# A fused attention and two-MLP kernel: block products in phases of 4, 4 and 6 units, sums on VectorE, weight sums split later

## The chip, the cores and the metric

One Trainium2 chip, one core. The metric is the device time of one execution in microseconds (us). TensorE multiplies (PE in the rows; PEld its weight loads), VectorE (DVE), ScalarE (ACT) and GpSimd (POOL) do the rest, SyncE (SP) issues the DMAs. Each engine works through its own queue in order.

## The reference, cut to what matters

```python
def reference(q, k, v, moe_w_in, moe_w_out, moe2_w_gate, moe2_w_val, moe2_w_out, moe2_rms_g):
    x = attention(q, k, v)              # 4 x 8 heads, 576 tokens, window 128, distance bias
    x = heads_joined(x)                 # 2304 tokens x 512
    h = x @ moe_w_in                    # 512 x 2048
    x = (h * np.clip(h + 3, 0, 6) / 6) @ moe_w_out
    xn = x / np.sqrt(np.mean(x * x, -1, keepdims=True) + 1e-6) * moe2_rms_g
    g = xn @ moe2_w_gate                # 512 x 1536
    return (g / (1 + np.exp(-g)) * (xn @ moe2_w_val)) @ moe2_w_out
```

## The kernel before, in words

All products run in float32r on TensorE, and every operand is given as a high part (a rounded copy, made by ScalarE) and a low part (operand minus high part, made by VectorE). A product of two such pairs is three matmuls: high by high, high by low, low by high.

**First MLP with attention.** Six blocks of 384 tokens; a slot per 128 columns of the hidden layer, in which attention steps of a later block, ten to twenty matmuls each, are mixed in. In parts 3 to 5 of it (blocks 2 to 4; p in the code) most slots end with a *turn* of the second MLP's weights (`W2.turn`): a piece of 128x512 comes as 64-bit words, is converted by `convert` on VectorE and ScalarE, and goes back to DRAM: the two input matrices as they are (kinds 0 and 1), the output matrix (kind 2) split into high and low. When both pieces of a pair of output-weight chunks are there, GpSimd forms four sums of their halves (S1 to S4), and in the next two turns ("late") ScalarE and VectorE split these and SyncE stores them. `TURNS` holds the order of the pieces; a pair of chunks takes six turns, and two extra turns stand in part 5.

**Second MLP.** Tokens come in three sets of 768 (s = 0, 1, 2), the hidden layer in twelve chunks of 128; a *group* i = 12 s + m is one chunk of one set, 36 in all. A group computes gate and value by seven block products of six matmuls each (a form of Strassen's method, Winograd's), into three PSUM banks; the banks alternate between even and odd groups. Its steps, in code order: product 0, ScalarE copies it (`s1`, line 919); product 1, VectorE adds (`u`, line 922); product 2 on top of product 0, ScalarE's Silu (925); product 3 on top of product 1, VectorE adds (928); product 4, VectorE (931); product 5, which overwrites the bank of products 1 and 3, VectorE (933), Silu (934); product 6, VectorE (937) and the multiplication 938, which gives the group's hidden values g. So product 2 waits for `s1`, product 3 for the add of 922, product 5 for that of 928, product 6 for that of 931.

Other work is placed by `job(i, place, ...)` at fixed places of group i: "start", "silu" (behind line 925), "sum" (behind 928), "silu 2" (behind 934), "end" (behind 938), or a number, which is a unit of the phase or outputs behind the group.

Set 0's output product is plain (`outputs`, behind groups 2, 4, 6, 8, 11 and 12). The input weights' block operands are made during the last part of the first MLP and groups 2 to 8 (`Parts`: load, four GpSimd sums, high, low, stores). Sets 1 and 2 have their output product in *rounds* of four groups, six rounds, 0 to 5, again by seven block products: SEQUENCE c a g b e f d, each of one factor from the weights (A.. or S.., fetched from DRAM into three rooms in turn, line 1069) and one from g (B.. or T..). T1 to T4 are differences of g's blocks (`Round.sum`, line 1054); each block's high part is line 1057, its low part line 1060; p is the half of the round's groups it comes from (0: the first two, 1: the last two). A *unit* is one block product for one half d of the output columns: six matmuls (line 1076), then an eviction into a running total: ScalarE copies in a set's first round (1105), VectorE adds otherwise (1107; e and f always). b adds into a's PSUM tile and d into e's. A round's units run in two phases: eight behind its sixth following group (c a g b, behind i0 + 5), six behind i0 + 7 (e f d). Behind the last group the last round's 14 units run in a row. After a unit pair the factor three places further in SEQUENCE is fetched. `ROUND_JOBS` and `FINAL_JOBS` (last round) place the sums and parts, relative to i0 + 4. At the end of a set, adds of totals and the stores follow (1123, 1126), on GpSimd for set 1 and VectorE for set 2.

In the trace group 8 begins at 634.0 us, 13 at 696.2, 14 at 703.5, 16 at 718.3, 17 at 726.5, 24 at 823.9, 28 at 874.3, 35 at 960.7.

## Time and profile before

| | |
|---|---|
| median of 3 runs | 998.02 us (997.67 to 998.17) |
| the profiled execution | 998.81 us, its span 996.8 us |
| TensorE, matmuls | 941.9 us busy, 94% |
| VectorE | 687.1 us, 69% |
| ScalarE | 478.0 us, 48% |
| GpSimd | 253.0 us, 25% |
| mean granted TensorE clock | 0.987 |

The span runs from the first to the last instruction; the time also holds what lies around it. Busy shares are means over stages with different limits, so a wait must be looked at in its own stage. A clock of 1.0 is 2.4 GHz, and the other level, 1.2 GHz, shows as a mean below 1.0 where it held for a part of a stretch.

### The profile page before, as it was taken

How to read it: one execution, taken by the hardware profiler on the slowest of the kernel's cores; microseconds unless marked ns; L12 is line 12 of the kernel's file. 1: busy time of each engine (PE TensorE's matmuls, PEld its weight loads, DVE VectorE, ACT ScalarE, POOL GpSimd, SP SyncE). 2: the span in 40 equal slices, each digit the busy share in tenths (PEclk: the TensorE clock that was granted, in tenths of full speed). 3: DMA queues.
4: the chain of work that ended last, by engine and by line, in shares of the span. 5: the costliest groups of instructions: out<-in, count | busy, mean ns of one | idle time of the engine just before them, and what ended most of it. 6: DMA issues, size and time to landing. Idle time of an engine off the chain costs nothing.

```text
span 996.8 us, 15304 instructions
## 1 busy us (share of the span) xinstructions
PE 941.9 (94%) x5408; PEld 844.2 (85%) x5408; DVE 687.1 (69%) x1433; ACT 478.0 (48%) x1049; POOL 253.0 (25%) x390
## 2 busy tenths in 40 slices
PE   7899999999989999989999999999989888988897
PEld 4677888888877888878998999998979888988887
DVE  6788666556878778876567657777545677564667
ACT  6799556455556556654455444331224332223231
POOL 4333022232324344333323323200020202050210
PEclk9899999999999999999999999999999999999999
DMA  7546211024666574761454778675785565666526
GB/s 237 185 166 243 116 38 41 30 70 143 211 220 209 173 228 144 248 213 74 148 201 187 276 260 317 238 273 195 272 300 192 192 212 204 243 240 216 208 85 211
DMA packets 90860, 190.79 MB, mean 191 GB/s; under 512 B 6432, under 2 KB 66848, under 8 KB 87584
## 3 DMA queue, kind: packets, MB, share of 16 engines
q1 hardware_dynamic: 90784, 189.82, 55.1%
q8 instruction: 42, 0.69, 0.3%
q14 instruction: 34, 0.28, 0.1%
HBM read 139.46 MB, written 50.33 MB: 190 GB/s over the span
## 4 chain that ended last, share of the span: by engine, by line
PE 67%; DVE 14%; ACT 7%; DMA 5%; issue 4%; POOL 2%; SPq 0%; ACTq 0%; DVEq 0%; POOLq 0%
PE ps_o L559 14%; PE ps_h L546 14%; PE ps_o L911 9%; PE ps_y L1076 6%; PE ps_S L911 5%; PE ps_A L911 5%; PE ps_y L961 5%; PE ps_h L911 3%; DMA u<-w 3%; PE ps_av L480 2%; DVE u L1060 2%; DMA wraw<-w 2%; PE ps_t L462 2%; DVE wx L187 1%; PE ps_s L419 1%
## 5 line engine op out<-in xcount | busy, mean ns | idle before, releaser
L559 PE MATMUL ps_o<-w,g 128*128 128x512 f32 x864 | 225.6, 404 | 2.0 <-DVE w L191 1.8
L546 PE MATMUL ps_h<-xs,w 128*128 128x384 f32 x1152 | 220.5, 339 | 2.1 <-DVE t L786 2.0
L546 PEld LDWEIGHTS ps_h<-xs,w 128*128 128x128 f32 x1152 | 202.3, 188 | 8.9 <-DVE t L786 3.3
L559 PEld LDWEIGHTS ps_o<-w,g 128*128 128x128 f32 x864 | 157.3, 189 | 41.4 <-issue 5.6
L786 DVE SCALAR_TENSOR_TENSOR t<-t,ps_h 128x384 f32<-128x384 f32 x96 | 53.0, 552 | 92.5 <-ACT t L785 92.5
L1054 POOL TENSOR_TENSOR u<-u 128x384 f32<-128x384 f32 x33 | 39.2, 1207 | 247.6 <-DVE u L1054 237.9
L1076 PE MATMUL ps_y<-u 128*128 128x384 f32 x424 | 85.3, 340 | 6.0 <-DMA u<-w 6.0
L785 ACT ACTIVATE t<-ps_h,three 128x384 f32<-128x384 f32 x96 | 55.2, 575 | 74.6 <-PE ps_h L546 68.5
L911 PE MATMUL ps_o<-S,tw 128*128 128x384 f32 x336 | 69.6, 351 | 15.1 <-DVE u L922 14.8
L1076 PEld LDWEIGHTS ps_y<-u 128*128 128x128 f32 x424 | 75.2, 191 | 8.2 <-issue 4.5
L911 PEld LDWEIGHTS ps_o<-S,tw 128*128 128x128 f32 x336 | 61.8, 196 | 17.5 <-DVE u L922 16.9
L448 ACT ACTIVATE t<-t,m 128x128 f32<-128x128 f32 (+1 forms) x144 | 61.2, 427 | 31.0 <-DVE t L440 15.9
L791 ACT CAST g<-t 128x384 fp32r<-128x384 f32 x96 | 49.3, 514 | 52.3 <-DVE t L786 50.7
L934 ACT ACTIVATE r<-r 128x384 f32<-128x384 f32 x36 | 18.9, 526 | 115.6 <-DVE r L933 115.6
L450 POOL TENSOR_SCALAR r<-den 128x2 f32<-128x2 f32 x72 | 27.7, 385 | 180.5 <-ACT t L448 178.5
L797 DVE TENSOR_TENSOR g<-t,g 128x384 fp32r<-128x384 f32 x96 | 57.2, 596 | 22.8 <-ACT g L791 22.5
L469 POOL TENSOR_SCALAR_AFFINE_SELECT pt<-pt 128x256 f32<-128x256 f32 x82 | 36.1, 442 | 89.2 <-ACT pt L467 86.4
L451 POOL TENSOR_TENSOR r<-r,minus 128x2 f32<-128x2 f32 x72 | 56.4, 783 | 6.0
L1060 DVE TENSOR_TENSOR u<-u 128x384 fp32r<-128x384 f32 x64 | 42.2, 688 | 14.6 <-ACT u L1057 14.5
L961 PE MATMUL ps_y<-wo,g 128*128 128x512 f32 x216 | 50.0, 389 | 0.0
L462 PE MATMUL ps_t<-ident,t 128*128 128x128 f32 x190 | 35.5, 290 | 13.9 <-DVE t L456 7.2
L180 ACT ACTIVATE wx<-wraw 128x512 f32<-128x512 f32 (+1 forms) x52 | 42.7, 821 | 11.5 <-DMA wraw<-w 11.5
(169 smaller groups left out, 1744.2 us busy)
## 6 DMA issues: line engine op xcount, KB each, us to landing
tw<-t SPq DMA_DIRECT2D x52, 896.0 KB, 6.3
wraw<-w SPq DMA_DIRECT2D x36, 512.0 KB, 4.6
wraw<-w SPq DMA_DIRECT2D x16, 1024.0 KB, 9.1
u<-s SPq DMA_DIRECT2D x48, 256.0 KB, 5.5
t<-th SPq DMA_DIRECT2D x12, 896.0 KB, 4.1
t<-tl SPq DMA_DIRECT2D x12, 896.0 KB, 4.2
u<-w SPq DMA_DIRECT2D x36, 256.0 KB, 4.0
b<-wx SPq DMA_DIRECT2D x24, 256.0 KB, 3.6
```

The source lines that it names most:

```text
L448: act.activation(p, p, AF.Exp, bias=self.m[:, a : a + 1], scale=-1.0, accum_out=self.den[:, a : a + 1])
L451: pool.tensor_tensor(self.r, self.r, minus, ALU.pow)
L462: pe.transpose(self.ps[:, a, c], self.t[:, a, c * P : (c + 1) * P], ident)
L546: pe.matmul(ps[:, : n * P], lhsT=w[:, a, c * P : (c + 1) * P], rhs=xs[c][:, b, : n * P], start=(k == 0), stop=(k == 3 * KC - 1),)
L559: pe.matmul(o, lhsT=g[:, a, i * P : (i + 1) * P], rhs=w[:, b], start=(m == first and a == 0 and b == 0), stop=(m == last and a == 1),)
L785: act.activation(r[:, :nq], ps[:, :nq], AF.Relu, bias=three)
L786: vec.scalar_tensor_tensor(out=r[:, :nq], in0=r[:, :nq], scalar=6.0, in1=ps[:, :nq], op0=ALU.min, op1=ALU.mult)
L797: vec.tensor_sub(g[:, 1, :nq], r[:, :nq], f32(g[:, 0, :nq]))
L911: pe.matmul(ps, lhsT=w[a][:, k, c * P : (c + 1) * P], rhs=x[:, b, c], start=(start and j == 0), stop=(j == 5), skip_group_check=True,)
L961: pe.matmul(ps, lhsT=gs[i + k][:, a, t // 3, t % 3 * P : (t % 3 + 1) * P], rhs=wo[i + k][:, b], start=(k == 0 and a == 0 and b == 0), stop ...
L1060: vec.tensor_sub(self.part(name, p, 1), self.at(name, p), f32(self.part(name, p, 0)))
L1076: pe.matmul(ps, lhsT=w[:, p, a, d * P : (d + 1) * P], rhs=self.part(name, p, b), start=(p == j == 0 and k not in CHAINED), stop=(p == 1 an ...
```

## The change

Five things are changed.

- A round's units run in three phases: c and g behind group i0 + 5, a and b behind i0 + 6, e, f and d behind i0 + 7. c and a change their PSUM tiles with each other's kind: c, a, b, e, d use the fixed pair, g and f the pair of the next group's banks.
- All sums of g (T1 to T4) are on VectorE; none is left on GpSimd. The places of sums and parts are new, and the rooms of the parts (`slot`) follow them.
- The sums of the output weights are stored unsplit in the first MLP. In the second, behind the "end" of groups 4 to 15 one is loaded (`load_sum`), and at "silu" of groups 5 to 16 it is split and stored (`split_sum`). The two extra turns go, and `TURNS` begins each pair of chunks with the output weights.
- The last round runs a b, c g, e f d; of set 1's and set 2's last adds, C12's is on GpSimd.
- Some steps of the operands of set 2 (`turn(s)` with s = 1) move by a place or two.

```diff
+TURNS = [(m + i, k) for m in range(0, M2, 2) for i, k in ((0, 2), (0, 0), (1, 2), (0, 1), (1, 0), (1, 1))]
+FACTORS = {"c": ("S4", "B22"), "g": ("S3", "T3"), "a": ("A11", "B11"), "b": ("A12", "B21"), "e": ("S1", "T1"), "f": ("S2", "T2"), "d": ("A22", "T4")}
+SPLIT_AT = 5
 ROUND_JOBS = {
...
-    (0, "silu"): [("sum", "vec", "T1", 0), ("sum", "vec", "T1", 1), ("sum", "pool", "T3", 0), ("sum", "pool", "T3", 1), ("high", "B21", 0), ("high", "B21", 1)],
+    (0, "silu"): [("sum", "T3", 0), ("sum", "T3", 1), ("low", "B22", 1), ("high", "T3", 0), ("high", "T3", 1)],
...
-UNITS = {5: "c0 c1 a0 a1 g0 g1 b0 b1".split(), 7: "e0 e1 f0 f1 d0 d1".split()}
+UNITS = {5: "c0 c1 g0 g1".split(), 6: "a0 a1 b0 b1".split(), 7: "e0 e1 f0 f1 d0 d1".split()}
...
         def turn(self):
-            late, self.late = self.late[:1], self.late[1:]
-            for m, parity, x in late:
-                t = wcpool.tile([P, 2, DM], F32R, tag="wt", name="w", bufs=1)
-                act.copy(t[:, 0], x)
-                vec.tensor_sub(t[:, 1], x, f32(t[:, 0]))
-                sp.dma_start(out=self.sums[m][:, parity], in_=f32(t))
...
                 run.send(t)
-                self.begin()
+                if m % 2 == 0:
+                    self.begin()
                 next(run)
...
-                    self.late = [(m // 2, i, x) for i, x in enumerate(self.x)]
+                    for parity, y in enumerate(self.x):
+                        sp.dma_start(out=self.sum32[m // 2][:, parity], in_=y)
                     self.x = []
+                    self.begin()
+
+        def load_sum(self, i):
+            self.late[i] = ypool.tile([P, DM], F32, tag="y", name="ws")
+            sp.dma_start(out=self.late[i], in_=self.sum32[i // 2][:, i % 2])
+
+        def split_sum(self, i):
+            x = self.late.pop(i)
+            high, low = (ypool.tile([P, DM], F32R, tag="y", name="wt") for _ in range(2))
+            act.copy(high, x)
+            vec.tensor_sub(low, x, f32(high))
+            for k, y in enumerate((high, low)):
+                sp.dma_start(out=self.sums[i // 2][:, i % 2, k], in_=f32(y))
...
-            if not last and (p == 3 and m > 3 or p > 3 and m % 4 != 2 or p == 5 and m in (2, 6)):
+            if not last and (p == 3 and m > 3 or p > 3 and m % 4 != 2):
                 W2.turn()
...
-        def sum(self, on, name, p):
+        def sum(self, name, p):
...
-            on.tensor_sub(self.at(name, p), self.at(a, p), self.at(b, p))
+            vec.tensor_sub(self.at(name, p), self.at(a, p), self.at(b, p))
...
+        def order(self):
+            return [SEQUENCE[k] for k in ((2, 3, 0, 1, 4, 5, 6) if self.final else range(7))]
...
-                    p, tag = own[k not in CHAINED.values()][d]
+                    p, tag = own[k in "gf"][d]
...
-                            on.tensor_add(total(x, d), total(x, d), total("V", d))
+                            (pool if x == "C12" else on).tensor_add(total(x, d), total(x, d), total("V", d))
...
-            job(i + 9, 5, x.later, "S4", 2)
-            job(i + 9, 6, x.high, 1)
-            job(i + 10, "silu 2", x.later, "S3", 3)
-            job(i + 10, "end", x.low, 1)
+            job(i + 9, 3, x.later, "S4", 2)
+            job(i + 9, 3, x.high, 1)
+            job(i + 10, "silu 2", x.low, 1)
+            job(i + 10, 3, x.later, "S3", 3)
...
+    for i in range(M2):
+        job(SPLIT_AT - 1 + i, "end", W2.load_sum, i)
+        job(SPLIT_AT + i, "silu", W2.split_sum, i)
...
-    for off in UNITS:
+    for off in (6, 5, 7):
         x.phase(off, x.i0 + off)
```

Where instructions stand now is shown at three places. The first is ScalarE in group 8, from the copy `s1` on (`th` is a high part of the input weights); before:

```order
L919 COPY s_7007<-ps_h 128x384
L948 CAST g<-t 128x768
L925 ACTIVATE r<-ps_h 128x384
L316 CAST th<-tx 128x1024
L934 ACTIVATE r<-r 128x384
L316 CAST th<-tx 128x768
```

and now:

```order
L938 COPY s_7003<-ps_h 128x384
L967 CAST g<-t 128x768
L944 ACTIVATE r<-ps_h 128x384
L335 CAST th<-tx 128x1024
L308 CAST wt<-ws 128x512
L953 ACTIVATE r<-r 128x384
```

The cast of a weight sum (`wt` from `ws`) stands behind the one of `th`. VectorE in the same group, before:

```order
L922 TENSOR_TENSOR u<-s_7007,ps_A 128x384
L950 TENSOR_TENSOR g<-t,g 128x768
L928 TENSOR_TENSOR u<-s_7007,ps_A 128x384
L931 TENSOR_TENSOR t<-u,ps_S_7006 128x384
L933 TENSOR_TENSOR r<-u,ps_A 128x384
```

and now:

```order
L941 TENSOR_TENSOR u<-s_7003,ps_A 128x384
L969 TENSOR_TENSOR g<-t,g 128x768
L309 TENSOR_TENSOR wt<-ws,wt 128x512
L947 TENSOR_TENSOR u<-s_7003,ps_A 128x384
L950 TENSOR_TENSOR t<-u,ps_S_7002 128x384
L952 TENSOR_TENSOR r<-u,ps_A 128x384
```

The subtraction of that split stands between the group's first two adds (922 and 928 before, 941 and 947 now).

The second place is VectorE from the end of group 16 to the first add of group 17 (low parts are `u<-u` of line 1060, now 1084; a sum is line 1054, now 1078); before, while GpSimd has its six sums in the same stretch:

```order
L928 TENSOR_TENSOR u<-s_7713,ps_A 128x384
L931 TENSOR_TENSOR u<-u,ps_S_7712 128x384
L933 TENSOR_TENSOR r<-u,ps_A 128x384
L1060 TENSOR_TENSOR u<-u 128x384 x2
L937 TENSOR_TENSOR u<-u,ps_S_7712 128x384
L938 TENSOR_TENSOR u<-u,r 128x768
L1060 TENSOR_TENSOR u<-u 128x384 x3
L922 TENSOR_TENSOR u<-s_7797,ps_o_7795 128x384
```

and now:

```order
L947 TENSOR_TENSOR u<-s_7777,ps_A 128x384
L950 TENSOR_TENSOR u<-u,ps_S_7776 128x384
L952 TENSOR_TENSOR r<-u,ps_A 128x384
L956 TENSOR_TENSOR u<-u,ps_S_7776 128x384
L957 TENSOR_TENSOR u<-u,r 128x768
L1084 TENSOR_TENSOR u<-u 128x384 x2
L941 TENSOR_TENSOR u<-s_7858,ps_o_7856 128x384
```

Two low parts stand between the multiplication and the next group's first add instead of three. The third place is VectorE from group 34 on; before, group 35 follows at once:

```order
L928 TENSOR_TENSOR u<-s_9586,ps_A 128x384
L931 TENSOR_TENSOR u<-u,ps_S_9585 128x384
L933 TENSOR_TENSOR r<-u,ps_A 128x384
L1060 TENSOR_TENSOR u<-u 128x384 x2
L937 TENSOR_TENSOR u<-u,ps_S_9585 128x384
L938 TENSOR_TENSOR u<-u,r 128x768
L1060 TENSOR_TENSOR u<-u 128x384
L1054 TENSOR_TENSOR u<-u 128x384
L922 TENSOR_TENSOR u<-s_9663,ps_o_9661 128x384
```

and now, with the evictions of a0 a1 b0 b1 (line 1135) behind it:

```order
L947 TENSOR_TENSOR u<-s_9617,ps_A 128x384
L950 TENSOR_TENSOR u<-u,ps_S_9616 128x384
L952 TENSOR_TENSOR r<-u,ps_A 128x384
L1078 TENSOR_TENSOR u<-u 128x384
L1084 TENSOR_TENSOR u<-u 128x384 x2
L956 TENSOR_TENSOR u<-u,ps_S_9616 128x384
L957 TENSOR_TENSOR u<-u,r 128x768
L1078 TENSOR_TENSOR u<-u 128x384 x2
L1135 TENSOR_TENSOR u<-u,ps_y 128x384 x4
```

Three jobs stand at "silu 2", and two sums between the multiplication and the first eviction.

## Rows read from the trace of the kernel before

**Rows 1.** Waits of TensorE, whole run: waiter, releaser: us, times, longest.

```profile
PE ps_o L911 <- DVE u L922: 14.9, 7, 3.4
PE ps_y L1076 <- DMA u<-w: 7.5, 6, 1.9
PE ps_t L462 <- ACT pt L467: 6.4, 6, 2.0
```

**Rows 2.** Busy time by windows of 20 us, with PEclk, the granted clock.

```profile
780.00:800.00 20.00, 15.13 (x77) 14.33 (x75) 12.69 (x19) 4.28 (x8) 3.17 (x3) 0.91 0.61 223
```

**Rows 3.** Timeline of TensorE: start, us, instruction, count [idle before, releaser].

```profile
703.54 1.21 PE L911 MATMUL ps_h<-A,tw 128*128 128x384 f32 x6
...
710.91 1.21 PE L911 MATMUL ps_S<-A,tw 128*128 128x384 f32 x6
...
868.09 6.40 PE L1076 MATMUL ps_y<-u 128*128 128x384 f32 x36
874.33 1.22 PE L911 MATMUL ps_h<-A,tw 128*128 128x384 f32 x6
...
991.44 0.34 PE L1076 MATMUL ps_y<-S,u 128*128 128x384 f32 x1
```

**Rows 4.** Timelines of VectorE, ScalarE and TensorE in group 13, which begins at 696.16.

```profile
698.53 0.56 DVE L922 TENSOR_TENSOR u<-s,ps_o 128x384 f32<-128x384 f32 x1 [1.49 <-PE ps_o L911]
699.52 0.49 ACT L925 ACTIVATE r<-ps_S 128x384 f32<-128x384 f32 x1 [1.57 <-PE ps_S L911]
700.58 0.56 DVE L928 TENSOR_TENSOR u<-s,ps_o 128x384 f32<-128x384 f32 x1 [1.49 <-PE ps_o L911]
701.43 1.22 PE L911 MATMUL ps_o<-A,tw 128*128 128x384 f32 x6
702.68 0.56 DVE L933 TENSOR_TENSOR r<-u,ps_o 128x384 f32<-128x384 f32 x1 [0.50 <-PE ps_o L911]
703.74 0.55 DVE L937 TENSOR_TENSOR u<-u,ps_o 128x384 f32<-128x384 f32 x1 [0.50 <-PE ps_o L911]
704.40 0.96 DVE L938 TENSOR_TENSOR u<-u,r 128x768 f32<-128x768 f32 x1
```

**Rows 5.** Timelines of VectorE, GpSimd and TensorE in group 17, which begins at 726.45.

```profile
726.07 1.02 DVE L1060 TENSOR_TENSOR u<-u 128x384 fp32r<-128x384 f32 x2
726.79 2.87 POOL L1054 TENSOR_TENSOR u<-u 128x384 f32<-128x384 f32 x2 [1.42 <-ACT r L934]
728.71 3.10 DVE L1060 TENSOR_TENSOR u<-u 128x384 fp32r<-128x384 f32 x3
732.33 2.38 PE L911 MATMUL ps_o<-S,tw 128*128 128x384 f32 x12 [2.58 <-DVE u L922]
```

**Rows 6.** Groups by line, shapes apart: count | busy us, mean ns | idle before.

```profile
L1054 POOL TENSOR_TENSOR u<-u 128x384 f32<-128x384 f32 x33 | 39.2, 1207 | 247.6 <-DVE u L1054 237.9 <-ACT r L934 5.8 <-DVE u L1060 3.8
L266 DVE TENSOR_TENSOR w<-wx,w 128x512 fp32r<-128x512 f32 x12 | 8.9, 743 | 5.5 <-ACT w L265 5.5
L265 ACT CAST w<-wx 128x512 fp32r<-128x512 f32 x12 | 7.4, 615 | 2.2 <-DMA w<-w 1.7 <-DMA s<-w 0.5
```

**Rows 7.** Timeline of ScalarE: group 8 (from 634.02), and three casts in a row.

```profile
638.70 1.05 ACT L316 CAST th<-tx 128x1024 fp32r<-128x1024 f32 x1 [0.82 <-POOL tx L309]
...
771.66 1.34 ACT L1057 CAST u<-u 128x384 fp32r<-128x384 f32 x3
```

**Rows 8.** Timelines of GpSimd and VectorE around the beginning of group 28.

```profile
872.04 3.93 POOL L1123 TENSOR_TENSOR u<-u 128x384 f32<-128x384 f32 x4 [34.59 <-DVE u L1107]
875.00 2.68 DVE L1060 TENSOR_TENSOR u<-u 128x384 fp32r<-128x384 f32 x2
```

**Rows 9.** Timelines of ScalarE and TensorE in part 5 of the first MLP.

```profile
436.33 0.67 ACT L180 ACTIVATE wx<-wraw 128x512 f32<-128x512 f32 x1 [1.59 <-DMA wraw<-w]
437.79 0.62 PE L462 MATMUL ps_t<-ident,t 128*128 128x128 f32 x2 [2.02 <-ACT pt L467]
```

**Rows 10.** DMA issues: instruction, count, KB each, median us to landing.

```profile
u<-s SPq DMA_DIRECT2D x48, 256.0 KB, 5.5
```

More of the change, by code (lines that the diff above doesn't have):

```diff
@@ L241, in __init__ @@
             self.sums = [dram.tile([P, 2, 2, DM], F32, tag=f"s2_{m}", name=f"s2_{m}") for m in range(M2 // 2)]
-            self.x, self.late = [], []
+            self.sum32 = [dram.tile([P, 2, DM], F32, tag=f"s1_{m}", name=f"s1_{m}") for m in range(M2 // 2)]
+            self.x, self.late = [], {}
         def load(self):
@@ L1019, in fused_kernel @@
     class Round:
-        all = {}
+        all, free = {}, [0, 1, 2, 3]
         def __init__(self, s, q):
@@ L1029, in __init__ @@
             self.ps = {}
+            x = self.slot = dict(zip(OPERANDS, Round.free))
+            x["T1"], x["T2"], x["T4"] = x["B22"], x["T3"], x["B11"]
+            Round.free = [x["B21"], x["T1"], x["T4"], x["T2"]]
             for i in range(ROUND):
@@ L1086, in plan @@
                     for f, *args in jobs_:
-                        job(i + at[0], at[1], getattr(self, f), *[{"vec": vec, "pool": pool}.get(x, x) for x in args])
+                        job(i + at[0], at[1], getattr(self, f), *args)
                 return
@@ L1090, in plan @@
                 for f, *args in jobs_:
-                    job(i + at[0], at[1], getattr(self, f), *[{"vec": vec, "pool": pool}.get(x, x) for x in args])
+                    job(i + at[0], "end" if self.r == 0 and at[0] < 0 and at[1] != "silu" else at[1], getattr(self, f), *args)
         def phase(self, off, by):
@@ L1108, in phase @@
                 if d:
-                    i = 7 * self.r + SEQUENCE.index(k) + 3
+                    i = 7 * self.r + self.order().index(k) + 3
                     if i // 7 < len(rounds):
-                        rounds[i // 7].fetch(SEQUENCE[i % 7])
+                        rounds[i // 7].fetch(rounds[i // 7].order()[i % 7])
                 do(by, j)
@@ L1157, in turn @@
             job(i + 7, 2, x.high, 0)
-            job(i + 8, "silu 2", x.low, 0)
-            job(i + 9, 5, x.later, "S4", 2)
-            job(i + 9, 6, x.high, 1)
-            job(i + 10, "silu 2", x.later, "S3", 3)
-            job(i + 10, "end", x.low, 1)
+            job(i + 7, 4, x.low, 0)
+            job(i + 9, 3, x.later, "S4", 2)
+            job(i + 9, 3, x.high, 1)
+            job(i + 10, "silu 2", x.low, 1)
+            job(i + 10, 3, x.later, "S3", 3)
             for k in range(2, 7):
```

55 lines of the change are left out of this document (27 added, 28 removed), and 8 rows, old and new, of the table FINAL_JOBS.

## The prediction

> **What bounds the kernel now.** I read the busy table first (TensorE 94% of the span), then who waited for whom, then TensorE's order of time. TensorE sets the pace. Its own waits fall into two places. In the rounds it waits 14.9 us in 7 places for VectorE's `u` (line 922) and 7.5 us in 6 for a factor's DMA; in the first MLP with attention it waits for ScalarE's `pt` [rows 1]. Such a wait can cost twice: in the 20 us from 780 the granted clock is 0.91, that is 3.6 us at the lower of the two levels (1.2 instead of 2.4 GHz) behind a wait of 3.4 us, which is 1.8 us lost [rows 2].
>
> How much the rounds lose follows from the pitch. An undisturbed group is 710.91 - 703.54 = 7.37 us, six units are 874.33 - 868.09 = 6.24, one unit 1.04 [rows 3]. From group 14 to the last matmul stand 22 groups and 84 units: 162.1 + 87.4 = 249.5 us. The trace takes 991.61 - 703.54 = 288.1 [rows 3]. **So 38.6 us are lost there**: waits, restarts after them (about 0.1 each) and clock.
>
> Why VectorE is late is seen in group 17 (726.45). Two subtractions of one form take 1.02 us at 726.07; three of them at 728.71 take 3.10, while a GpSimd sum runs from 726.79; the `u` behind them comes late and TensorE idles 2.58 us [rows 5]. GpSimd's sums, 1.2 us each [rows 6], stand in VectorE's way. The Trainium skill ("SBUF — State Buffer", "Who interferes with whom") says that a VectorE instruction with two SBUF inputs and a GpSimd one that reads SBUF exclude each other, the second waiting for the whole of the first; the three subtractions agree.
>
> **The ruler.** Group 13 (696.16) is undisturbed [rows 4]. Relative to a group's start: `u0` (line 922) is due at 2.37; the first Silu at 3.36; `u1` (928) at 4.42, and the sixth product, which overwrites what `u1` reads, is due at 5.27; line 933 at 6.52; then, from the next start, 937 at 0.20 and the multiplication at 0.86, ending 1.8 (VectorE free again at 1.74). A VectorE step of 128x384 takes 0.55 but the next begins after 0.47 (two take 1.02), one of 128x768 0.96 and 0.88. So these jobs fit free: one between the multiplication and `u0` (0.63 us), three behind "silu" (1.6), one behind "silu 2". What goes beyond moves TensorE by its whole length, as it does nothing meanwhile.
>
> **What goes.** GpSimd's 33 sums [rows 6], six in each of five rounds and three in the last, become VectorE steps of 0.47. The factor waits go: with 4, 4 and 6 units a factor is fetched at least one group (7.4 us) before its use, against two block products (4.2 us) now. So of the 38.6 us I take out all, and put back what the new order still loses.
>
> The Trainium skill speaks against the move too: "Perfetto Trace Analysis", "Optimizing Scalar/DVE Operations", advises to hand work of a saturated VectorE to GpSimd, adding that the two share a port. By the advice alone 33 x 0.47 = 15.5 us would come on VectorE with nothing back. By the rows each of the three subtractions costs 0.5 more beside GpSimd, and VectorE is not saturated, so I go by the rows.
>
> **A. The split sums, groups 5 to 16.** Each group now has a ScalarE cast and a VectorE subtraction of 128x512 behind "silu" (0.62 and 0.74 us before, in another place [rows 6]). The cast can begin when the Silu is done (3.75) and ends at 4.37; the subtraction holds VectorE to 5.00, `u1` is 0.58 late, and the sixth product starts at about 5.6: 0.34 and a restart of 0.1. That is 0.45 in groups 9 to 14 (2.7). In 5 and 7 a low part follows at "sum" and the seventh product is late too: 0.7 each. In 6 and 8 ScalarE first has `th` (1.05), waiting for GpSimd in group 8 till 4.68 [rows 7]: the cast ends at 6.3, `u1` begins at 6.9: 2.3; in group 6, where it begins at 3.75, 1.3. Group 15 has a high part ahead: 0.9; in 16 two sums and two casts stand ahead: 1.0. Sum **9.6**. Bounds: 0 if `u1` had more slack than group 13 shows, 18 if every group were like 8.
>
> **B. Too many jobs before `u0`.** Group 16: five jobs after 1.74 end at 4.1, and ScalarE's cast of the group's own product, possible only after 1.8, delays the copy `s1`: 1.8. The second group of each of five rounds has two jobs (low parts of T3): 0.3 each, 1.5. Group 22: eviction, two low parts, a sum and one of 768 end at 2.97: 0.75. Group 24: between the multiplication and `u0` stand six evictions, five 768-wide low parts and four small jobs: 1.74 + 2.8 + 4.4 + 1.9 = 10.8, due 6.24 + 2.37 = 8.6: 2.35 (the old order lost 1.2 there). Group 28: GpSimd still does six output sums during the phase before it, from 3.95 us into it, four of them in 3.93; there two VectorE jobs take 2.68 instead of 1.02 [rows 8]. The old order had two such jobs, the new has four; I get 11.0 against 8.6: 2.3. Group 35: 0.3. Sum **9.0**.
>
> **C. ScalarE late with `s1`** (due 1.3, must end by 2.1). In group 34 five casts stand ahead of it from 0.2 on; three take 1.34 us [rows 7], five some 2.2, and the copy begins at about 2.3: 0.8; in groups 18 and 30 0.3 each. **1.4.**
>
> **D. b waits for a.** In the old phase four units stood between a0 and b0, which adds into the same PSUM tile; now it is two. b0 is due 2.08 after the phase begins, but a0's eviction stands behind the group's multiplication, 1.74 to 2.3: 0.35 in rounds 0 (there behind ScalarE's scaling) and 2; round 1 has a sum and a 768-wide step at "silu 2": 1.05; round 4 has three jobs there and two behind the multiplication, 1.74 + 0.8 + 0.9 + 0.55 = 4.0: 2.05. Round 3 evicts on ScalarE: nothing. In the last round a0 comes right behind d1 and needs the tile that d0 leaves; thirteen VectorE steps end at 1.74 + 6.1 = 7.85, due 6.24: 1.7. **5.5.** None of this is in the old trace; the lower bound is zero (an eviction in time), the upper twice this, if the backlog of one phase reaches the next group.
>
> **Clock.** Of the new waits four exceed 2 us. I take one stretch at the lower level: **1.8**; bounds 0 and four.
>
> Rounds: 9.6 + 9.0 + 1.4 + 5.5 + 1.8 = 27.3 put back, 38.6 taken out: **11.3 gained**.
>
> **E. First MLP with attention.** Twelve casts and subtractions leave it; before them VectorE waits 5.5 us for ScalarE [rows 6]. The two extra turns of part 5 go as well: behind one of them ScalarE waits 1.59 us for a weight's DMA and TensorE 2.02 [rows 9]. Against it, six odd turns now wait for their own cast before the next conversion begins. I take 2.0 for that wait and 2.5 of the other 4.4 us of `pt` waits and their like: **4.5 gained**, between 0 and 8. GpSimd's sums there are unchanged; SyncE's queue gets two stores behind them, and its next load has a slot's time.
>
> **F. The end.** GpSimd takes two of VectorE's last six adds: 0.9 less on VectorE, or as much more if they exclude each other. Taken as 0.
>
> **Sum** against the profiled execution (998.81, span 996.8): 998.81 - 11.3 - 4.5 = 983.0. The median of the runs is 0.8 lower, so **982**.
>
> **Rivals.** (1) *The splits cost nothing*, since ScalarE and VectorE run a little earlier than group 13 shows, and phases recover a part of B to D: 9.6 and about 4 less, 968. For it: single windows are missed by only 0.2 to 0.6 us. Against: VectorE works in order, and `u1` stands behind the subtraction. 20%. (2) *VectorE becomes the bound*: a round has four groups of some 3.2 us, 14 evictions and 22 jobs of 0.47 on it, 30 of 44 us, so it is not full on average, but backlogs could run into each other: B and D double less what hides, 991. 9%. (3) *GpSimd was not the cause*: VectorE's slow steps stay as they are; then about 14 us of the waits remain, 996. The pairs taken alone speak against it. 5%. (4) *Slower: the loads of the split sums land late.* A load is issued only after the split before it (about 5.1 in its group) and is needed at 3.75 in the next: 6.0 us where no outputs stand between, in nine groups. A like load takes 5.5 us (median) [rows 10]. If it took 8, ScalarE, the Silu and TensorE behind it would lose 2 in nine groups, 18 in all: 1000. It decides from about 7.8 us on. 6%. The forecast itself: 60%, 976 to 988.
>
> **How the numbers follow.** Below 966 lies somewhat under half of (1), 8%; above 993 lie (3) and (4), 11%: the range 966 to 993 leaves out 2 in 10. A measurement of this kernel can tell 0.2% (2 us). Faster: forecast, (1), (2) and most of (3), 0.92; same 0.03; slower 0.05.
>
> **What would show it.** Right: no factor wait of TensorE; no VectorE step of 1.3 us but before group 28; twelve waits of 0.3 to 2.3 us at the sixth product of groups 5 to 16; waits at b0 in rounds 1 and 4 and at a0 of the last. Wrong: groups 9 to 14 at 7.37 us (A falls), factor waits that stay, or ScalarE waiting for the `ws` loads.

## The result, and the profile after

The change makes the kernel 1.5% faster: 982.99 us (median, 982.43 to 985.32) against 997.88 (997.67 to 998.17) in the same comparison, a ratio of 0.9855 (95% interval 0.9838 to 0.9872). The profiled execution took 985.32 us, the longest of the four. Line numbers from here on are those of the kernel after, if nothing else is said (911 is now 930, 922 is 941, 928 is 947, 1057 is 1081, 1060 is 1084, 1076 is 1104); experiments shift them by a few. First the page of after: busy times, and the lines of the chain that ended last.

```profile
span 983.6 us, 15380 instructions
PE 943.7 (96%) x5408; PEld 845.7 (86%) x5408; DVE 696.0 (71%) x1464; ACT 479.2 (49%) x1049; POOL 220.4 (22%) x359
...
PE ps_o L578 18%; PE ps_h L565 18%; PE ps_o L930 8%; PE ps_S L930 7%; PE ps_y L1104 7%; PE ps_A L930 5%; PE ps_y L980 5%; DMA ws<-s 3%; PE ps_av L499 3%; PE ps_h L930 3%; PE ps_t L481 2%; PE ps_s L438 2%; PE ps_s L429 1%; DVE wx L195 1%; ACT wx L188 1%
```

TensorE is still the bound; the part of the span in which it is not busy fell from 54.9 to 39.9 us. New is a DMA on the chain: `ws<-s`, the load of a weight sum. Waits of TensorE, whole run (waiter, releaser: us, times, longest), beside [rows 1]:

```profile
PE ps_A L930 <- DVE u L947: 11.4, 5, 6.5
PE ps_t L481 <- DVE t L475: 5.1, 3, 2.4
PE ps_y L1104 <- DVE u L1135: 4.5, 3, 2.0
PE ps_A L930 <- DVE u L941: 4.2, 4, 2.0
PE ps_t L481 <- ACT pt L486: 2.1, 3, 0.9
```

The 14.9 us for a group's first add (line 941) are down to 4.2, and no factor's DMA is waited for. In their place stand 11.4 us for its second add (947), 6.5 of them at one place, and 4.5 for an eviction (1135).

Where the time went is read best from the starts of ScalarE's copy `s1`, one in each group (all times in us; the last matmul is taken at its start):

| stretch | before | after | gained | predicted |
|---|---|---|---|---|
| start to group 0's copy | 547.0 | 535.0 | 12.0 | 4.5 |
| groups 0 to 4 | 57.7 | 57.4 | 0.3 | 0 |
| groups 5 to 13 | 100.1 | 116.4 | -16.2 | -7.25 |
| group 14 to the last matmul | 286.6 | 269.9 | 16.7 | 18.55 |
| last matmul to the end of the span | 5.4 | 5.0 | 0.4 | 0 |
| sum | 996.8 | 983.6 | 13.2 | 15.8 |

(Predicted, from its terms: of A's 9.6 us 7.25 lie in groups 5 to 13, so 27.3 - 7.25 = 20.05 of what was put back lies behind them, and 38.6 - 20.05 = 18.55.) **The total is right because two terms are wrong by nearly the same amount**: the first MLP gave 7.5 us more, the split sums took 9 us more. That they cancel is luck. The rounds came out within 2 us.

Group 6, where most of that was lost: ScalarE, VectorE, TensorE and SyncE's DMA issues, each from its own timeline.

```profile
602.92 1.05 ACT L335 CAST th<-tx 128x1024 fp32r<-128x1024 f32 x1
609.26 0.62 ACT L308 CAST wt<-ws 128x512 fp32r<-128x512 f32 x1 [5.29 <-DMA ws<-s]
...
609.91 0.69 DVE L309 TENSOR_TENSOR wt<-ws,wt 128x512 fp32r<-128x512 f32 x1 [6.36 <-ACT wt L308]
610.52 0.55 DVE L947 TENSOR_TENSOR u<-s,ps_A 128x384 f32<-128x384 f32 x1
...
604.27 0.34 PE L930 MATMUL ps_S<-S,tl 128*128 128x384 f32 x1
611.12 1.01 PE L930 MATMUL ps_A<-A,th 128*128 128x384 f32 x2 [6.52 <-DVE u L947]
611.92 0.52 PE L930 MATMUL ps_A<-A,tl 128*128 128x384 f32 x1
...
592.48 0.89 SPq L715 DMA_DIRECT2D x2raw<-x  x1
...
597.89 0.59 SPq L303 DMA_DIRECT2D ws<-s  x1
```

Read it backwards. The sixth product (611.12) waits 6.52 us for the add of line 947. That add stands behind the subtraction 309, the subtraction waits for the cast 308, and the cast for the load, which was issued at 597.89 and landed at 609.2: 11.3 us, with the 1.5 MB of x2raw (the tokens of the second set) issued 5.4 us ahead of it. Behind the wait a matmul takes 0.5 instead of 0.34 us. Windows of 20 us show that TensorE's clock was lower there (first column behind the length: TensorE's busy time; last three: granted clock, DMA share, GB/s), and three more stretches of the kind:

```profile
600.00:620.00 20.00, 13.48 (x58) 12.24 (x57) 9.38 (x12) 9.34 (x13) 6.87 (x8) 0.83 0.69 252
640.00:660.00 20.00, 19.84 (x92) 18.02 (x93) 15.40 (x23) 5.42 (x9) 0.00 (x0) 0.91 0.83 299
820.00:840.00 20.00, 18.03 (x93) 17.43 (x93) 15.67 (x29) 5.55 (x12) 0.00 (x0) 0.91 0.50 165
940.00:960.00 20.00, 18.04 (x93) 17.32 (x92) 15.21 (x30) 5.80 (x13) 0.00 (x0) 0.91 0.25 78
```

### The profile page after: what moved, and what is told of

Its sections match the earlier page's. It is cut to its first block, busy times and chain, and to the rows that moved or that the text cites. A ratio compares the mean times of both kernels' runs of the same rounds, so it can differ in the third digit from the quotient of the medians.

```text
span 983.6 us, 15380 instructions
## 1 busy us (share of the span) xinstructions
PE 943.7 (96%) x5408; PEld 845.7 (86%) x5408; DVE 696.0 (71%) x1464; ACT 479.2 (49%) x1049; POOL 220.4 (22%) x359
## 4 chain that ended last, share of the span: by engine, by line
PE 78%; DVE 10%; ACT 5%; DMA 3%; issue 2%; POOL 1%; SPq 0%; ACTq 0%; DVEq 0%; POOLq 0%
PE ps_o L578 18%; PE ps_h L565 18%; PE ps_o L930 8%; PE ps_S L930 7%; PE ps_y L1104 7%; PE ps_A L930 5%; PE ps_y L980 5%; DMA ws<-s 3%; PE ps_av L499 3%; PE ps_h L930 3%; PE ps_t L481 2%; PE ps_s L438 2%; PE ps_s L429 1%; DVE wx L195 1%; ACT wx L188 1%
## 5 line engine op out<-in xcount | busy, mean ns | idle before, releaser
L1151 POOL TENSOR_TENSOR u<-u 128x384 f32<-128x384 f32 x6 | 7.2, 1237 | 332.3 <-DVE u L1135 332.3
L467 ACT ACTIVATE t<-t,m 128x128 f32<-128x128 f32 (+1 forms) x144 | 61.1, 426 | 29.4 <-DVE t L459 15.8
L953 ACT ACTIVATE r<-r 128x384 f32<-128x384 f32 x36 | 18.9, 526 | 106.0 <-DVE r L952 106.0
L930 PE MATMUL ps_o<-S,tw 128*128 128x384 f32 x336 | 66.7, 340 | 0.3 <-DVE t L950 0.3
L930 PEld LDWEIGHTS ps_o<-S,tw 128*128 128x128 f32 x336 | 58.9, 188 | 2.4 <-DVE u L941 1.6
L488 POOL TENSOR_SCALAR_AFFINE_SELECT pt<-pt 128x256 f32<-128x256 f32 x82 | 39.7, 487 | 76.6 <-ACT pt L486 73.7
L980 PEld LDWEIGHTS ps_y<-wo,g 128*128 128x128 f32 x216 | 41.3, 192 | 8.3
L452 DVE CUSTOM_DVE_ANT_0 t<-ps_s,rel 128x256 f32<-128x256 f32 (+2 forms) x128 | 45.1, 393 | 4.4 <-PE ps_s L438 4.4
L1081 ACT CAST u<-u 128x384 fp32r<-128x384 f32 x66 | 32.1, 512 | 30.2 <-DVE u L1078 14.3
```

What stands on the lines that cost most here:

```text
L452: vec.tensor_tensor_reduce(out=self.t[:, a, c0:], in0=s[:, c0:], in1=(rel_split if self.i in SPLITS else rel)[:, c0:], scale=2.0 ** (-8.0 ...
L467: act.activation(p, p, AF.Exp, bias=self.m[:, a : a + 1], scale=-1.0, accum_out=self.den[:, a : a + 1])
L930: pe.matmul(ps, lhsT=w[a][:, k, c * P : (c + 1) * P], rhs=x[:, b, c], start=(start and j == 0), stop=(j == 5), skip_group_check=True,)
L980: pe.matmul(ps, lhsT=gs[i + k][:, a, t // 3, t % 3 * P : (t % 3 + 1) * P], rhs=wo[i + k][:, b], start=(k == 0 and a == 0 and b == 0), stop ...
```

## The experiments

Each ran on the same chip as a few runs of the kernel before, whose median there was 999 to 1001.5 us, so ratios are compared, and what a term is worth is read from the steps between copies (a group's step runs from its copy `s1` to the next group's). A step is that of one profiled execution. All start from the kernel after, if not said otherwise.

**1. Splits back in the first MLP.**

```diff
         def turn(self):
+            late = [self.late.pop(k) for k in sorted(self.late)[:1]]
+            for m, parity, x in late:
+                t = wcpool.tile([P, 2, DM], F32R, tag="wt", name="w", bufs=1)
+                act.copy(t[:, 0], x)
+                vec.tensor_sub(t[:, 1], x, f32(t[:, 0]))
+                sp.dma_start(out=self.sums[m][:, parity], in_=f32(t))
...
-    for i in range(M2):
-        job(SPLIT_AT - 1 + i, "end", W2.load_sum, i)
-        job(SPLIT_AT + i, "silu", W2.split_sum, i)
```

> The changed kernel with one part undone: the weight sums are split in the turns of the first MLP again (in the two turns behind the four sums), so nothing is loaded or split in groups 4 to 16. The new order of turns and the missing extra turns stay. Reading of the changed kernel's trace: group 0 begins 12.0 us earlier than before, groups 5 to 16 lose some 19 us. Theory 1 (the splits are what the groups lose, and about half of what the first MLP gained): groups 5 to 16 without a wait at the sixth product, group 0 about 6 us later than in the changed kernel, 970 us. Rival 2 (all that the first MLP gained came from taking the splits out): group 0 back at 545, 976 us. Rival 3 (none of it did; the order of turns and the two extra turns were all): group 0 at 534, 964 us. Rival 4 (groups 5 to 16 lose by something else, loads of the operands for instance): no gain there, 983 or more.

968.77 us, ratio 0.9684 (0.9646 to 0.9722). Group 0's copy is at 539.5, and groups 5 to 15 take 115.6 us (115.8 before), against 134.6 after; group 16's step falls from 9.4 to 8.3. So the moved splits cost 20 us where they went. Group 0's copy comes 4.5 us later than in the kernel after, and 5.5 to 7 later than in the seven other runs that leave its first MLP as it is (532.5 to 534.0); so much was freed where they came from: **this part of the change by itself loses some 14 us**. The two ratios differ by 17 us, with intervals that leave 12 to 23. Theory 1 holds.

**2 and 3. Earlier loads; and the subtraction elsewhere.** Experiment 2 writes the low part over the sum, so that the next load finds a free buffer, and issues the load a group earlier. Experiment 3 also moves the subtraction behind the add of line 952 (last line).

```diff
-        job(SPLIT_AT - 1 + i, "end", W2.load_sum, i)
+        job(SPLIT_AT - 1 + i, "start", W2.load_sum, i)
...
+        job(SPLIT_AT + i, "silu 2", W2.sub_sum, i)
```

> The changed kernel with the load of each weight sum issued at the start of the group before its split instead of at that group's end; so that the buffers suffice, the low part is written over the sum. Cast and subtraction stay where they are. Theory 1 (the loads landed late in groups 6, 8 and 14): ScalarE waits for no ws load; the sixth product of group 6 waits about 1.3 us instead of 6.5, of group 8 1.2 to 2.3 instead of 2.5, of group 14 0.2 instead of 1.4, and the stretch at the lower clock behind group 6 goes: 11 us gained, 972 us. Rival 2 (the landing is only seen there, and the casts of th and the subtraction of 128x512 hold the sixth product): the waits stay, 983 us.

979.49 us, ratio 0.9789 (0.9738 to 0.984). Only part of it came true: group 6's step falls from 24.8 to 22.3 us, and its sixth product still waits 3.9 us, where 1.3 was expected; 14's step stays at 9.0. In group 8 the cast waits for no DMA any more, and the sixth product still waits 2.05 us (2.49 after). ScalarE's cast in group 6 and SyncE's issue of the store that it waits for, in experiment 2:

```profile
604.17 0.62 ACT L307 CAST wt<-ws 128x512 fp32r<-128x512 f32 x1 [2.65 <-DMA s<-ws]
...
593.75 0.32 SPq L310 DMA_DIRECT2D s<-ws  x1
```

Now it isn't the load that is late but the store of the split before: issued at 593.75, it holds the buffer until 604.17, 10.4 us. The five transfers issued next behind x2raw take 10 to 13 us each there, so other buffers only let another of them end last.

> As the kernel with the early loads, and the subtraction of each split moved from in front of the group's second add (line 947) to behind the add of line 952 (the place called silu 2); the cast stays. Theory 1 (the subtraction in front of line 947 is what makes the sixth product late): no wait at the sixth product in groups 5 to 16, of VectorE's gap of 0.50 us before line 956 the subtraction of 0.61 takes all, which the slack before the next group's first add hides; against the early loads alone 6 us less, 966 us. Rival 2 (the subtraction moves the lateness to the next group's first add): waits at the third product of the next group of 0.3 to 0.7 us in their place, no gain against the early loads, 972 us.

968.33 us, ratio 0.9687 (0.9642 to 0.9731). No wait for the second add is left, and the steps of groups 10, 13 and 14 are back at 7.4 to 7.5 us (7.8, 7.8 and 9.1 after). Rival 2 came true at one place: the first add behind copy 9 is waited for, 1.0 us, and group 9's step is 8.7 instead of 7.8. Group 6 still takes 18.7 us, since the late store now delays, by way of the cast and the subtraction, the outputs behind the group:

```profile
PE ps_y L982 <- DVE y L989: 2.9, 2, 2.5
```

**4. x2raw's load one group earlier.**

```diff
-        job(i + 5, "start", x.load)
+        job(i + (5 if s else 4), "start", x.load)
```

> The changed kernel with the load of the second set's tokens (x2raw, 1.5 MB, one DMA) issued at the start of group 4 instead of group 5; all else stays. Theory 1 (the weight sum of group 6 lands 11.3 us after its issue because it stands behind that load and the stores around it): ws lands in about 5 us in group 6, the sixth product there waits about 1.3 us instead of 6.5 and the stretch at the lower clock behind it goes, 7 us gained, 976 us; group 8 stays as it is. Rival 2 (the other loads and stores around it, 0.9 MB each, are enough): group 6 waits as long, 983 us.

977.59 us, ratio 0.9772 (0.975 to 0.9793). Group 6's step falls from 24.8 to 19.9 us, 8 stays at 20.0, as expected; but the load in group 6 takes 7.2 us and not 5, and the sixth product waits 2.5 and not 1.3. The cast in group 6, and the time from issue to landing of all transfers of `ws`, in this kernel (in the kernel after the last line reads 3.2/4.9/11.3):

```profile
604.39 0.62 ACT L308 CAST wt<-ws 128x512 fp32r<-128x512 f32 x1 [1.29 <-DMA ws<-s]
...
DMA to landing us min/median/max: 3.3/5.0/7.5
```

So x2raw ahead in the queue is the larger half of group 6's loss (4.9 of 9.2 us); the other loads and stores there (0.9 and 1 MB) leave a landing that is still 1.3 us too late.

**5. Sums on GpSimd again, in the new places.**

```diff
-            vec.tensor_sub(self.at(name, p), self.at(a, p), self.at(b, p))
+            on = vec if name == "T1" or (self.final and p) else pool
+            on.tensor_sub(self.at(name, p), self.at(a, p), self.at(b, p))
```

> The changed kernel with the sums T2, T3 and T4 of rounds 0 to 4, and of the first half of the last round, on GpSimd again (33 of them, as before); their places stay as changed. Theory 1 (GpSimd's sums hold VectorE's steps with operands in SBUF): VectorE steps of 1 us and more for a pair's half beside each sum, more waits of TensorE for line 941 and at the phases, 5 to 14 us lost, 988 to 997 us. Rival 2 (GpSimd was not the cause, and VectorE gains 33 steps of 0.47 us): no slow steps, 976 to 983 us.

982.21 us, ratio 0.9822 (0.9784 to 0.986): no difference from the kernel after can be told. Copy 17 to 28 takes 132.1 us (after 131.9). 28 to 35 takes 78.2 (after 81.4; but 79.8 in experiments 1 to 4, whose instructions there are the same, so half of that difference isn't the sums'). GpSimd and VectorE around group 16 in this kernel:

```profile
728.31 3.71 POOL L1079 TENSOR_TENSOR u<-u 128x384 f32<-128x384 f32 x3 [0.65 <-ACT u L1082]
...
726.84 1.24 DVE L1079 TENSOR_TENSOR u<-u 128x384 f32<-128x384 f32 x1
728.00 0.54 DVE L941 TENSOR_TENSOR u<-s,ps_A 128x384 f32<-128x384 f32 x1
728.47 1.26 DVE L1085 TENSOR_TENSOR u<-u 128x384 fp32r<-128x384 f32 x1
```

VectorE's steps beside a sum still take 1.24 and 1.26 instead of 0.56 us. From group 14 on ten of its 128x384 steps take over 0.8 us, 13 in the kernel before, three in the one after. They cost where the first add stands behind them (TensorE waits 1.5 us for it instead of 0.8 in group 16, 2.65 instead of 1.97 in 24), but VectorE has 33 steps less, and the wait at b0 in round 4 falls from 1.96 to 0.90. The half of theory 1 on the steps holds, its price doesn't.

**6 and 7. The same sums in the old kernel.** Both start from the kernel before. The first only gives T2 and T4 a later place, still on GpSimd; the second makes them there on VectorE ("vec" for "pool" in the last line).

```diff
-    (0, "end"): [("low", "B21", 1), ("sum", "pool", "T2", 0), ("sum", "pool", "T2", 1), ("sum", "pool", "T4", 0), ("sum", "pool", "T4", 1), ("high", "T3", 0), ("high", "T3", 1)],
+    (0, "end"): [("low", "B21", 1), ("high", "T3", 0), ("high", "T3", 1)],
+    (1, "silu"): [("sum", "pool", "T2", 0), ("sum", "pool", "T2", 1), ("sum", "pool", "T4", 0), ("sum", "pool", "T4", 1)],
```

> The kernel before with one edit: GpSimd's four sums T2 and T4 of each round stand behind the first Silu of the second group (place silu of i0 + 5) instead of at the end of the first, so that they no longer run beside the three low parts that VectorE has in front of that group's first add. They stay on GpSimd. Theory 1 (in the old order these sums held VectorE there, three low parts 3.10 us): the three take 1.5 us, the wait for line 922 in five groups (2.6 to 3.4 us) falls to about 1.0, 8 us gained and up to 5 of clock, 985 to 990 us. Rival 2 (three low parts in that place are too many with or without GpSimd, and it is not what holds them): the waits stay, 998 us.

999.68 us, ratio 0.9997 (0.9983 to 1.0012), and no test at all: GpSimd has nothing else queued, its operands are there, so it makes the sums when it did before, and VectorE's three low parts take as long.

```profile
726.74 2.87 POOL L1055 TENSOR_TENSOR u<-u 128x384 f32<-128x384 f32 x2 [1.43 <-ACT r L935]
...
728.65 3.11 DVE L1061 TENSOR_TENSOR u<-u 128x384 fp32r<-128x384 f32 x3
```

> The kernel before with one edit: the sums T2 and T4 of rounds 0 to 4 are made by VectorE, behind the first Silu of the round's second following group (place silu of i0 + 5), instead of by GpSimd from the end of the first. In the run that only gave them another place GpSimd still made them at the same time, since it had nothing else to do and their data were there, so that run told nothing of this. Now GpSimd has nothing to do beside the three low parts of T3 and B21 in front of that group's first add. Theory 1 (GpSimd held VectorE there): the three low parts take 1.5 us instead of 3.1, the wait for line 922 falls from 2.6 to about 1.0 in five groups, and the stretches at the lower clock behind it shrink: 8 to 12 us gained, 988 to 992 us where before has 1000 on that chip. Rival 2 (the low parts are slow for another reason): they stay at 3.1 us, 998 to 1000 us. Rival 3 (the waits go, but the phase behind loses as much, since the factors' loads then are what ends last): waits of line 922 shorter, factor waits longer by as much, 997 to 1000 us.

988.88 us, ratio 0.9891 (0.986 to 0.9921). The same three low parts, and the waits of TensorE (beside [rows 5] and [rows 1]):

```profile
727.17 1.49 DVE L1061 TENSOR_TENSOR u<-u 128x384 fp32r<-128x384 f32 x3
...
PE ps_y L1077 <- DMA u<-w: 6.6, 6, 1.9
PE ps_o L912 <- DVE u L923: 6.0, 7, 1.7
```

3.11 us have become 1.49, the waits for the first add have gone from 14.9 to 6.0, and the factor waits have hardly moved. So GpSimd did hold VectorE there: theory 1. It was 10 us of the old time by the medians, and 7.5 by the profiled executions from group 14 to the last matmul.

**8. Phases of eight and six again.** The jobs of the second phase move to the end of its group. This kernel leaves out one condition, that g has read T3's room before T2's parts are put into it; so g multiplies T2's high part, and its totals of C22 are wrong. The work is the same in number.

```diff
-UNITS = {5: "c0 c1 g0 g1".split(), 6: "a0 a1 b0 b1".split(), 7: "e0 e1 f0 f1 d0 d1".split()}
+UNITS = {5: "c0 c1 a0 a1 g0 g1 b0 b1".split(), 7: "e0 e1 f0 f1 d0 d1".split()}
...
-    for off in (6, 5, 7):
+    for off in (5, 7):
```

> The changed kernel with the units in phases of 8 and 6 again (c a g b behind the sixth following group, e f d behind the eighth, the old PSUM tiles and the old order of the last round); all sums stay on VectorE, and the new places of sums and parts stay, but for those that stood in the second phase, which go to the end of the same group. Known so far: with the sums on GpSimd again the changed kernel is as fast as without, so the engine of the sums is not what the rounds gained by. Theory 1 (the phases took out the factor waits, 7.5 us, and brought the waits of b for a, 4.5 us; the places took out the rest): factor waits of 1 to 2 us back, no wait at b0, 987 us. Theory 2 (the phases are most of what the rounds gained): late adds of line 941 of 2 to 3 us again at the beginning of the groups behind the phases, 998 us. Rival 3 (the phases do nothing): 979 to 983 us.

995.46 us, ratio 0.9961 (0.9942 to 0.9979): 10.6 us of 998 lost against the kernel after. TensorE's waits from 715 us on, in this kernel:

```profile
PE ps_y L1103 <- DMA u<-w: 6.6, 4, 2.3
PE ps_A L929 <- DVE u L940: 4.0, 3, 2.0
PE ps_S L929 <- ACT s L937: 3.9, 2, 3.0
PE ps_y L1103 <- ACT u L1080: 2.3, 2, 1.1
```

The factor waits are back, and 6.2 us of waits for ScalarE besides. The time lies between theories 1 and 2, but these 6.2 us come from places and not from the phases as such. Twice g waits 1.1 us for the cast of T2's high part, which it reads only because of the condition left out (first line). And the copy of group 35, 3.0 us late, stands behind two casts that wait for four sums, jobs that this kernel moved to the end of group 34 (the copy of group 19, 0.9 us late, stands behind two moved casts and two other steps):

```profile
747.51 2.38 PE L1103 MATMUL ps_y<-u 128*128 128x384 f32 x12 [1.14 <-ACT u L1080]
...
957.63 2.33 DVE L1077 TENSOR_TENSOR u<-u 128x384 f32<-128x384 f32 x4
...
958.81 1.15 ACT L1080 CAST u<-u 128x384 fp32r<-128x384 f32 x2 [2.65 <-DVE u L1077]
959.86 0.47 ACT L937 COPY s<-ps_S 128x384 f32<-128x384 f32 x1
```

Taken off, they leave some 4 of the 10.6 us for the phases as such, an estimate, which is nearer to theory 1's balance: 6.6 us of factor waits go, 4.5 us of waits for evictions come.

| copies | undisturbed | before | 7 | 8 | after | 5 |
|---|---|---|---|---|---|---|
| 17 to 28 | 124.8 | 147.9 | 143.0 | 141.8 | 131.9 | 132.1 |
| 28 to 35 | 74.5 | 88.6 | 85.5 | 82.3 | 81.4 | 78.2 |

(Undisturbed: 11 groups of 7.37 and 42 units of 1.04 us [rows 3]; 7 groups and 22 units.) From before to 8 stand the new places and the engine, 12.4 us; from 8 to after the phases and the places that go with them, 10.9.

**9 and 10. What the first MLP gained besides the splits.** The two extra turns put in again; or the old order of the turns.

```diff
-            if not last and (p == 3 and m > 3 or p > 3 and m % 4 != 2):
+            if not last and (p == 3 and m > 3 or p > 3 and m % 4 != 2 or p == 5 and m in (2, 6)):
```

```diff
-TURNS = [(m + i, k) for m in range(0, M2, 2) for i, k in ((0, 2), (0, 0), (1, 2), (0, 1), (1, 0), (1, 1))]
+TURNS = [(m + k // 2, k % 2) if k < 4 else (m + k - 4, 2) for m in range(0, M2, 2) for k in range(6)]
```

> The changed kernel with the two extra turns of the old kernel in part 5 of the first MLP (slots 2 and 6); as the pieces are as many as before, the turns only come earlier and the last two find nothing to do. Known so far: group 0's copy s1 is at 547.0 us in the kernel before, at 533 to 535 in the changed kernel, and at 539.5 with the splits in the turns of the first MLP, so the splits are some 5.5 of the 12 to 13 us that the first MLP gained. Theory 1 (the extra turns are most of the rest): TensorE idles 2 us or more again in one or two slots of part 5, and the clock drops there: group 0's copy at 537 to 539 us, 987 us. Rival 2 (the order of the turns is the rest): nothing changes, 983 us.

> The changed kernel with the old order of the turns (both input pieces of two chunks, then the two pieces of the output matrix); the splits stay in the second MLP and no extra turns are made. Theory 1 (order is nothing, the extra turns are the rest): group 0's copy at 533 to 535 us, 983 us. Rival 2 (order is what the first MLP gained besides the splits): group 0's copy at 538 to 541 us, 988 us.

983.22 us (ratio 0.984, 0.9808 to 0.9871) and 990.34 us (0.9907, 0.9879 to 0.9935). Group 0's copy is at 533.3 with the extra turns and at 539.6 with the old order. So the extra turns are nothing, and the order is some 5 to 7 us: rival 2 of each. The windows of the same two stretches in before, after, 1 and 10, in that order:

```profile
280.00:330.00 50.00, 46.24 (x289) 40.08 (x288) 41.66 (x104) 30.19 (x77) 19.66 (x36) 1.00 0.68 224
430.00:480.00 50.00, 47.42 (x279) 41.35 (x279) 31.27 (x73) 23.93 (x55) 12.27 (x23) 0.97 0.44 145
```

```profile
280.00:330.00 50.00, 49.33 (x305) 42.93 (x304) 42.69 (x104) 31.21 (x79) 24.62 (x42) 1.00 0.63 205
430.00:480.00 50.00, 50.00 (x303) 44.75 (x302) 32.04 (x71) 23.96 (x56) 13.55 (x25) 1.00 0.41 138
```

```profile
280.00:330.00 50.00, 46.31 (x287) 39.88 (x287) 41.18 (x101) 30.59 (x77) 21.25 (x37) 1.00 0.56 187
430.00:480.00 50.00, 50.00 (x302) 44.45 (x301) 33.70 (x75) 25.09 (x58) 14.06 (x26) 1.00 0.51 170
```

```profile
280.00:330.00 50.00, 48.51 (x301) 42.65 (x302) 40.59 (x103) 31.28 (x80) 20.93 (x38) 1.00 0.61 196
430.00:480.00 50.00, 47.98 (x288) 42.39 (x289) 30.76 (x69) 23.30 (x55) 16.75 (x30) 1.00 0.44 149
```

TensorE's first column says it: with the splits (before, 1) it idles 3.7 us in the first stretch, with the old order (before, 10) 2.0 to 2.6 in the second. Over 230 to 530 us the idle time is 11.3 us before, 6.8 with the splits, 6.9 with the old order, 1.3 after.

**11 and 12. A better version.** Experiment 3 with the twelve splits in groups that have room, none in 6 and 8, and GpSimd making T2, T3, T4 in round 4 and the first half of the last. The second adds g first in the last round (the last two lines of the diff) and T1 of rounds 0 and 2 on GpSimd, which in the first stays on VectorE.

```diff
-SPLIT_AT = 5
+SPLIT_AT = (5, 7, 9, 10, 11, 12, 13, 14, 15, 16, 19, 20)
...
-            vec.tensor_sub(self.at(name, p), self.at(a, p), self.at(b, p))
+            gp = self.r in (0, 2) if name == "T1" else self.r == 4 or self.final and p == 0
+            (pool if gp else vec).tensor_sub(self.at(name, p), self.at(a, p), self.at(b, p))
...
+    UNITS[5] = "g0 g1 c0 c1".split()
+    for off in (5, 6, 7):
```

> A version made of what the runs showed: early loads and late subtractions as in the third experiment, the twelve splits in groups 5, 7, 9 to 16, 19 and 20, so none in groups 6 and 8, where loads and stores are slow; and in round 4 and the first half of the last round GpSimd has the sums T2, T3, T4, since with them on GpSimd the step from group 34 to 35 was 1.4 us shorter. Theory 1: against the third experiment group 6 gains 3.2 us, groups 8 and 9 2.3, group 34 1.4, groups 19 and 20 lose up to 0.6: 962 us. Rival 2 (the splits in groups 19 and 20 delay rounds 1 and 2, whose factors need them): 968 us or more.

962.26 us, ratio 0.9618 (0.96 to 0.9636). Groups 6 and 8 take 15.6 us each, as before the change; groups 5 to 15 together 115.9 (115.8 before), though nine of the twelve splits stand there. In places with room they cost nothing that can be measured.

> The best version so far (962.3 us) with two more edits that try two terms of the prediction. In the last round g comes first (g c, a b, e f d), whose PSUM tiles are the next group's banks, so that no first unit of the phases needs the tile that d0 has just left: the wait of 1.7 us at a0 goes. The sums T1 of rounds 0 and 2 are made by GpSimd, two of the steps less that stand in front of the first add of groups 16 and 24: the 2.0 us wait of group 24 falls by 1 us with its clock, that of group 16 by 0.4. Theory 1: 959 us. Rival 2 (VectorE's backlog moves to the next unit, c0 or a0): the wait appears two or four units later, 961 us. Rival 3 (GpSimd's sums slow the low parts beside them there): group 24 as before or later, 962 to 963 us.

**958.86 us, ratio 0.9591 (0.9562 to 0.962)**, theory 1. Group 24's step falls from 11.2 to 9.3 us and its wait from 1.98 to 1.28. Most of the step is clock: in experiment 2, with the wait as long as ever (1.98), the 20 us from 810 have a granted clock of 1.00, and the step is 9.6. What TensorE still waits for VectorE in the second MLP:

```profile
PE ps_A L932 <- DVE u L943: 2.7, 3, 1.3
PE ps_y L1107 <- DVE u L1138: 2.6, 3, 0.9
PE ps_A L932 <- DVE u L949: 0.7, 1, 0.7
```

The longest is 1.3 us; no stretch of 20 us from 580 to 940 shows a granted clock below 1.0.

## Why the prediction was right, and where it wasn't

Forecast 982, measured 982.99: the sign, the size and the range are right, and the plan of the sum (a ruler for the group, what goes, what comes back) held in the rounds. That the total is within 1 us is luck: A and E are both far off, and cancel. By its steps:

- **What goes, 38.6 us.** (The last matmul's row ends at 991.78, not 991.61; it would be 38.7.) Taken out whole for two causes, both of which are real: the sums beside the low parts are 7.5 to 10 us (7), the phases 4 to 11 with the places that go with them (8). But the step "33 sums become VectorE steps" isn't by itself what freed the time. In the new order the sums cost as much on GpSimd as on VectorE (5); the two waits named under 5 suggest that what counts is how many slow steps stand in front of a first add, but no run changed that alone. Rival 3 falls for the old order and is half right for the new. The Trainium skill ("SBUF — State Buffer", "Who interferes with whom") has a VectorE instruction with two SBUF inputs and a GpSimd one that reads SBUF exclude each other; 3.11 us that become 1.49 agree. Its hint ("Perfetto Trace Analysis", "Optimizing Scalar/DVE Operations") that work moved between the two might not help fits the 33 sums in the new order (5), and not T2 and T4 in the old one, whose move to VectorE gained 10 us (7).
- **A, 9.6 us: 20.** That is 18.9 in groups 5 to 15 and 1.1 in 16. The ordinary case was about right: 9 loses nothing, 10 to 13 lose 0.3 to 0.5 (0.45 taken). What was missed stands in three groups: 6 loses 9.2 (I had 1.3), 8 loses 4.3 (2.3), 14 loses 1.7 (0.45). In 6 and 14 that is rival 4's mechanism, a late landing, which I had put at 6% and apart from the forecast, with one delay for nine groups. In 8 the wait, 2.5 us, is about A's own (2.05 in experiment 2, where the cast waits for no DMA); the rest of its loss is one of the stretches at the lower clock. The trace of before could have placed the late landing: x2raw's load, two stores of 0.9 MB and a load of 1 MB are issued around groups 5 to 8 there too, and a store of 256 KB (line 603 there, `x<-yt`) that is issued 3 us behind x2raw takes 9.2 us:

```profile
L603 SPq DMA_DIRECT2D x<-yt x18: 513/550/628, 210.8 to 607.8; - x18
...
DMA to landing us min/median/max: 2.5/3.1/9.2
```

  The failed step is "a like load takes 5.5 us (median)": the median held (4.9), the maximum of 11.3 decided.
- **B, C.** TensorE's waits in after are 1.3 us in group 16 (1.8 predicted), 0.2 in 22 (0.75), 2.0 in 24 (2.35), 1.2 in 28 (2.3), 0.2 in 34 (0.8): the right places, but 4.9 us for these five instead of 8.0, and the eight of 0.3 each don't show. So B, C and D, put at 15.9 us, are 9.4 us of waits. The rounds, too, came out within 2 us by some luck: the clock (two stretches, 3.6 us at most) and losses that stand in no wait made it up. 12 bears out B's reading of group 24: less in front of the add, 0.7 us less of wait.
- **D.** 0.84 us in round 1 (1.05 predicted), 1.96 in round 4 (2.05), 1.74 at a0 of the last round (1.7), nothing in rounds 0 and 2 (0.35 each). The best of the terms, since it counts steps behind a known time:

```profile
944.16 0.68 PE L1104 MATMUL ps_y<-A,u 128*128 128x384 f32 x1 [1.96 <-DVE u L1135]
...
963.73 2.55 PE L1104 MATMUL ps_y<-u 128*128 128x384 f32 x13 [1.74 <-DVE u L1135]
```

- **Clock, 1.8 us.** One stretch was taken, four came: (0.17 + 3 x 0.09) x 20 = 8.8 us at most, for TensorE was idle in a part of them, and two of them are inside A's 20. One lies behind the late landing in group 6, three behind waits of 2 to 2.5 us that A, B and D had named, so there the term could have been counted. Nor does such a wait always bring it: behind b0's wait of 1.94 to 1.97 us in round 4 the clock fell here and in 9 and 10, and not in 1 to 4, and group 34's step is 15.6 us here and 14.0 there.
- **E, 4.5 us: 12.0**, or 13 to 14.5 by the seven runs with the same first MLP. The step that failed is halving the `pt` waits and charging 2 us for the turns of the odd chunks. The idle time of the stretch (230 to 530 us), 11.3 us, was to be read first; nearly all of it went, half by the splits (1) and half by the order of the turns (10). I credited the extra turns instead, for the wait of 2.02 us behind one [rows 9]; put back they cost nothing (9).
- **F.** 0 forecast; from the last matmul on 5.4 us became 5.0.
- **Its signs.** No factor wait: right. Waits at b0 and a0: right. VectorE steps of 1.3 us only before group 28: right for the rounds (1.37 and 1.25 for two there). Waits of 0.3 to 2.3 at the sixth product: those of 5, 7 and 9 to 13 are 0.2 or less, one is 6.5. ScalarE waiting for the `ws` loads, a sign of being wrong, came in groups 6, 8 and 14.

What stays open: how much of the 12.4 us from before to 8 the single places of sums and parts are, beside what 7 shows for T2 and T4; and what the phases of eight would cost with their jobs in better places. No run took these apart.
